# Retention and mixture of experts on one core: ten chunks whole in place of nine, and a five-step lead for the first expert job

## Chip, cores and metric

The kernel runs on one core of a Trainium2 chip. The metric is the device time of one execution in microseconds (us), as the median of several runs; lower is better. A profile is one further execution, taken by the hardware profiler.

## What is computed

A retention layer (a decaying linear attention) over 4 sequences of 768 tokens with 8 heads of 64 features is followed by a mixture of experts: each of the 3072 tokens goes to the one of 8 experts that its logits choose, through two matrix products with a ReLU between them.

```python
for t in range(S):                       # retention, per batch b and head h
    state = gamma * state + outer(k[:, :, t], v[:, :, t])
    y[:, :, t] = scale * q[:, :, t] @ state
x = y as [3072, 512]                     # heads side by side
logits = x @ w_gate + modality_bias[modality_id]
e_idx = argmax(logits);  gate_w = softmax(logits)[e_idx]
for e in range(8):
    h = relu(x[mask_e] @ w1[e])          # 512 -> 1024
    out[mask_e] = gate_w * (h @ w2[e])   # 1024 -> 512
```

## The kernel before

**Retention in chunks.** The 3072 tokens are 24 chunks of 128 tokens, six to a sequence (`NN` = 24, `NCH` = 6). A chunk needs the masked scores of its keys and queries, the state that earlier chunks left, the outputs from both, and the state for the next chunk. There are two forms:

- *Whole* (chunks 0 to 8, `n < WHOLE`, line 42): `whole_scores` (lines 281 to 290) makes 128x128 scores into two banks of PSUM, `whole_masked` masks them with two VectorE operations, `whole_state` (300) adds all 128 tokens to the state and copies it out with ScalarE (`keep_state`, 267), and `whole_out` (316) makes the output, again in two banks, and copies it as `yT` with two ScalarE operations. In matmul instructions of the trace that is 16 for scores, 16 for state, 16 for the state's part of the output (line 322) and 16 for the values' part (328): 64 a chunk.
- *In halves* (chunks 9 to 23): `scores`, `masked`, `grown` and `quarters` (211 to 378) treat two halves of 64 tokens, with matmuls of 64x64 on the four quarters of the array through `run` (line 276): 128 matmul instructions a chunk. One VectorE operation masks the scores, the state is copied out twice, and the output once.

The two forms lay the state out differently. `hand_over` (338) moves it with 16 matmul instructions on an identity (line 344) at the border, and copies the result out with ScalarE. The inputs are laid out on the host to the form of each chunk, and `decay_v` (1054) picks the factors for it. After either form `tokens_out` (381) transposes the output back to tokens (PE, line 388), and scales it: three VectorE operations (`lh`, `xs`, `lh`, line 396), one for the logits (`lg`, 417), and four on ScalarE (410).

**Routing.** After every third chunk `route` (1070) puts small steps on a list `todo`; `tick` (1066) runs one of them. For the second group of chunks (3 to 5) the steps are `a`, `a1`, `wait`, `first_b`, `wait`, `c`, `d`. Step `c` ends in the VectorE operation `ohs` (711); step `d` multiplies `ohs` on TensorE (`pt`, 721), and VectorE writes the list of jobs (`lst`, 725). From that list SyncE reads which rows and which expert the first job has.

**Jobs.** A job takes 256 tokens of one expert. Each weight tile is cut into a high part (ScalarE, `hi`, line 813) and a low part (VectorE, `lo`, 815). The rows are transposed on TensorE (`flip_x`; `xp`, 857) and split into `xTh` (ScalarE, 827) and `xTl` (VectorE, 828). Then come 96 matmuls of the first layer (872) and 48 of the second (887). Between them a job advances retention by five steps.

**Order of work.** PE, ScalarE, VectorE and SyncE run what the program issues in the order of the Python code. The generator `retention` (1140) yields three times in a whole chunk (after the next chunk's scores; after the tokens of the chunk before; at the end), twice in chunk 6, and twice in a chunk in halves. The main loop `everything` (1202) calls `tick` after each yield. At the first yield of chunk 8 the first list is written, and the first job is started there: loads of its rows and weights are issued. From then on the loop counts down:

```python
            if ahead is None:
                if min(EVENTS) in lists:
                    job = state_of[0] = start_job(jobs[0])
                    raw(job, 1, guess)
                    raw(job, 2)
                    ahead = AHEAD
            else:
                ahead -= 1
                if ahead in (2, 3):
                    cut(job, 1, 3 - ahead)
                if ahead == 1:
                    flip_x(job)
                if ahead == 0:
                    break
```

After the break the jobs run. The first layer's weights of a guessed expert are loaded earlier (from 29.8 us); `raw(job, 1, guess)` loads them again only if the guess was wrong.

Of the kernel before, what the change touches and what calls it, by code (L numbers as in the profile page):

```python
# [36 lines left out]

RUN = 8

AHEAD = 4  # L40

WHOLE = 9
EMPTY = 2 * NCAND
ZROW = NE * NT

# [10 lines left out]
def kernel(  # L56
# [194 lines left out]
    def grown(n, u):  # L251

        c = n % NCH
        if c == 0 and u == 0:
            pst[n // NCH] = bank(f"st_{n}")[:, : NG * D].rearrange("p (g e) -> p g e", g=NG)
        p = pst[n // NCH]
        kk = kvs[n][:, 0].rearrange("p (u g d) -> p u g d", u=2, g=NG)
        vd = values(n)
        return [
            (  # L260
                p[rows(j), g], kk[rows(j), u, g], vd[rows(j), u, g],
                c == 0 and u == 0 and g == 0,
            )
            for g in range(NG) for j in range(2)
        ]

    def keep_state(n, u):

        s = sts[n, u] = wk.tile([P, NG, D], F32, tag="s", name=f"s{u}_{n}", bufs=3)
        b = (n - 1 + u) // NCH  # L270
        nc.scalar.copy(s, pst.pop(b) if u and n % NCH == NCH - 1 else pst[b])

    def run(*lists):
        for i in range(0, max([0] + [len(l) for l in lists]), 2):
            for out_, l, r, start in sum((l[i : i + 2] for l in lists), []):
                nc.tensor.matmul(out_, l, r, start=start, stop=True, skip_group_check=True)  # L276
# [4 lines left out]
    def whole_scores(n):  # L281
        kt, qt = feat(n, 0), feat(n, 1)
        p = [bank(f"sc{j}_{n}").rearrange("p (g t) -> p g t", g=NG) for j in range(2)]
        for g in range(NG):
            for j in range(2):
                nc.tensor.matmul(  # L286
                    p[j][:, g], kt[rows(j), g], qt[rows(j), g], start=True, stop=True,
                    skip_group_check=True,
                )
        psc[n] = p  # L290

    def whole_masked(n):
        p = psc.pop(n)
        att[n] = me.tile([P, 2, NG, P], F32, tag=f"hi1{2 + n % 2}", name=f"a_{n}")
        for j in range(2):
            nc.vector.tensor_tensor(  # L296
                att[n][:, j], p[j], mask.unsqueeze(1).to_broadcast([P, NG, P]), op=ALU.mult
            )

    def whole_state(n):  # L300
# [11 lines left out]
        keep_state(n + 1, 0)  # L312
        if c == NCH - 2 and n + 1 < WHOLE:
            pst.pop(n // NCH)
# [690 lines left out]
    def raw(s, m, old=None):  # L1005
        load_weights(m, s["e"], None if old is None else old["e"])
# [47 lines left out]
    def decay_v(n):  # L1054
        vv = kvs[n][:, 1].rearrange("p (h e) -> p h e", h=H)
        by = decw if n < WHOLE else dec
        vds[n] = wk.tile([P, H, D], F32, tag="vd", name=f"vd_{n}", bufs=3)
# [82 lines left out]
    def retention(modi):  # L1140
# [5 lines left out]
        for n in range(NN):  # L1146
            if n < WHOLE:
                if (n + 1) % NCH:
# [4 lines left out]
                if listed:  # L1153

                    tokens_out(*prev)
                    route(min(EVENTS))
                if n + 1 < WHOLE:
                    whole_scores(n + 1)
# [5 lines left out]
                yield n  # L1164
                if n + 1 < WHOLE:
                    whole_masked(n + 1)
                else:
                    masked(n + 1)
                if prev is not None and not listed:
                    tokens_out(*prev)  # L1170
                    if n % GRP == 0:
                        route(n // GRP - 1)
                if n + 1 == WHOLE:
                    run(grown(n + 1, 0))
# [27 lines left out]
    def everything():  # L1202
# [17 lines left out]
        for n in ret:  # L1220
# [4 lines left out]
# [7 lines that stand above are left out]
# [141 lines left out]
```

## Time and profile before

| | us |
|---|---|
| median of 3 runs | 419.12 (417.92 to 419.55) |
| the profiled execution | 420.01 |
| its span in the trace | 418.2 |
| PE busy | 400.0 |
| VectorE (DVE) busy | 251.7 |
| ScalarE (ACT) busy | 207.3 |
| GpSimd (POOL) busy | 91.6 |

Times in the rows are us from the start of the span, unless marked ns. PE is TensorE, DVE VectorE, ACT ScalarE, POOL GpSimd, SP SyncE. The chain of waits follows the work that ended last back through what released it. "issue" is time in which the engine waited for nothing that the profile shows. PEclk is the TensorE clock that was granted: 1.00 is 2.4 GHz, 0.50 is 1.2 GHz.

### The profile page before, as it was taken

Reading aid. Unit: us, or ns where it says so; the run is one execution under the profiler, and the core shown is the slowest. Engines: PE = TensorE matmul, PEld = TensorE weight load, DVE = VectorE, ACT = ScalarE, POOL = GpSimd, SP = SyncE. Lnnn points to the kernel's source line nnn. Section 1 sums busy time; section 2 is a strip of 40 time slices with the busy share of each in tenths; the row PEclk is TensorE's granted clock in tenths of the full one; section 3 lists DMA queues with packets and bytes.
Section 4 is the critical chain, followed back from the end, with each engine's and each line's share of the span. In section 5 each row is a group of like instructions: output and inputs, shape, how many; then the busy total and the mean of one; then the engine's idle time right before and its main releaser. Section 6 shows DMA issues by size and latency. Waiting matters only on the chain.

```text
span 418.2 us, 12000 instructions
## 1 busy us (share of the span) xinstructions
PE 400.0 (96%) x4598; PEld 349.8 (84%) x4598; DVE 251.7 (60%) x605; ACT 207.3 (50%) x420; POOL 91.6 (22%) x118
## 2 busy tenths in 40 slices
PE   4998899999999999999999999999999999999994
PEld 3886799789879988988888988989898898968863
DVE  1876868746735767647745865967665573725600
ACT  1344276466545553655446537546454654626411
POOL 2425301412041115012501231210130101002001
PEclk9999899999999999999999999999999999999998
DMA  8999569986977664436920414842287589999001
GB/s 282 390 410 360 165 214 385 394 293 225 340 232 266 246 229 154 150 113 203 348 75 28 153 38 148 256 165 78 76 276 265 194 274 309 333 409 351 4 0 46
DMA packets 29978, 92.78 MB, mean 222 GB/s; under 512 B 4827, under 2 KB 4955, under 8 KB 29857
## 3 DMA queue, kind: packets, MB, share of 16 engines
q1 hardware_dynamic: 25360, 77.83, 53.7%
q0 software_dynamic: 4272, 13.67, 8.4%
q8 instruction: 37, 0.61, 0.6%
q10 hardware_dynamic: 288, 0.50, 0.3%
q14 instruction: 21, 0.17, 0.1%
HBM read 92.74 MB, written 17.48 MB: 264 GB/s over the span
## 4 chain that ended last, share of the span: by engine, by line
PE 82%; issue 8%; DMA 4%; DVE 3%; POOL 1%; POOLq 0%; ACT 0%; SPq 0%; ACTq 0%
PE h_e L872 28%; PE o_e L887 27%; PE x L388 6%; PE sc L276 3%; PE st L276 3%; PE h_s L872 3%; PE y L276 2%; PE xp_e L857 2%; DMA four<-in_w_dram 2%; PE sc L286 2%; PE y L328 2%; DMA cst<-in_consts_dram 1%; DVE a L296 1%; PE st L308 1%; PE y L322 1%
## 5 line engine op out<-in xcount | busy, mean ns | idle before, releaser
L815 DVE TENSOR_TENSOR lo_e<-raw,hi_e 128x1024 fp32r<-128x1024 f32 x80 | 100.7, 1260 | 72.9 <-ACT hi_e L813 65.3
L872 PE MATMUL h_e<-xTh,hi_e 128*128 128x256 f32 x320 | 91.9, 287 | 0.0
L872 PE MATMUL h_e<-xTh,lo_e 128*128 128x256 f32 x320 | 90.3, 282 | 0.0
L872 PE MATMUL h_e<-xTl,hi_e 128*128 128x256 f32 x320 | 90.3, 282 | 0.0
L813 ACT CAST hi_e<-raw 128x1024 fp32r<-128x1024 f32 x80 | 83.6, 1047 | 0.0
L887 PE MATMUL o_e<-hi_e,hTh 128*128 128x512 f32 x160 | 66.1, 413 | 0.0
L887 PE MATMUL o_e<-lo_e,hTh 128*128 128x512 f32 x160 | 63.2, 395 | 0.0
L887 PE MATMUL o_e<-hi_e,hTl 128*128 128x512 f32 x160 | 63.1, 394 | 0.0
L872 PEld LDWEIGHTS h_e<-xTh,hi_e 128*128 128x128 f32 x320 | 60.7, 190 | 0.7
L872 PEld LDWEIGHTS h_e<-xTh,lo_e 128*128 128x128 f32 x320 | 60.6, 189 | 0.3
L872 PEld LDWEIGHTS h_e<-xTl,hi_e 128*128 128x128 f32 x320 | 60.7, 190 | 0.0
L1058 POOL TENSOR_TENSOR vd<-kv,cst 128x512 f32<-128x512 f32 x24 | 28.2, 1174 | 99.6 <-DMA kv<-in_qkv_dram 40.4
L822 ACT ACTIVATE hTh<-h_e 128x256 fp32r<-128x256 f32 x80 | 30.8, 387 | 29.9 <-PE h_e L872 25.6
L410 ACT ACTIVATE xs<-x,cst 128x64 f32<-128x64 f32 x96 | 22.3, 315 | 45.2 <-DVE lh L396 26.0
L900 POOL DMA_INDIRECT out_dram<-o_e,xg_e x20 | 19.9, 994 | 112.2 <-ACT o_e L899 95.8
L823 DVE SCALAR_TENSOR_TENSOR hTl<-h_e,hTh 128x256 fp32r<-128x256 f32 x80 | 33.0, 419 | 14.3 <-ACT hTh L822 14.2
L887 PEld LDWEIGHTS o_e<-lo_e,hTh 128*128 128x128 f32 x160 | 30.1, 188 | 7.1
L899 ACT ACTIVATE o_e<-o_e,xg_e 128x512 f32<-128x512 f32 x20 | 13.8, 690 | 43.9 <-issue 27.3
L887 PEld LDWEIGHTS o_e<-hi_e,hTh 128*128 128x128 f32 x160 | 30.1, 188 | 6.1
L887 PEld LDWEIGHTS o_e<-hi_e,hTl 128*128 128x128 f32 x160 | 30.2, 189 | 5.5
L494 POOL DMA_INDIRECT x_dram<-xs,pos x24 | 26.9, 1119 | 33.9 <-DVE xs L460 12.8
L388 PE MATMUL x<-wgt,yT 128*128 128x144 f32 x192 | 31.2, 306 | 2.4 <-issue 1.8
(214 smaller groups left out, 659.5 us busy)
## 6 DMA issues: line engine op xcount, KB each, us to landing
raw<-in_w_dram SPq DMA_DIRECT2D x100, 512.0 KB
kv<-in_qkv_dram SPq DMA_DIRECT2D x24, 512.0 KB
four<-in_qkv_dram SPq DMA_DIRECT2D x19, 512.0 KB
xg_e<-x_dram SPq DMA_DIRECT2D x20, 257.0 KB
four<-in_w_dram SPq DMA_DIRECT2D x8, 512.0 KB
wb_u<-in_w_dram SPq DMA_DIRECT2D x16, 256.0 KB
kq<-in_qkv_dram SPq DMA_DIRECT2D x4, 512.0 KB
xg_s<-x_dram SPq DMA_DIRECT2D x4, 257.0 KB
```

The costliest lines, as they stand in the source:

```text
L276: nc.tensor.matmul(out_, l, r, start=start, stop=True, skip_group_check=True)
L388: nc.tensor.matmul(px[:, g], yT[:, 2 * u + g], wgt[:, 2 * u + g], start=(g == 0), stop=(g == 1), skip_group_check=True,)
L410: nc.scalar.activation(x[:, i], px[:, i // 2, rows(i % 2)], AF.Copy, scale=gain[:, c, 4 * u + i : 4 * u + i + 1],)
L494: ins = nc.gpsimd.indirect_dma_start(out=x_dram[:, :], out_offset=bass.IndirectOffsetOnAxis(ap=pos[:, i : i + 1], axis=0), in_=xs, in_offs ...
L813: nc.scalar.copy(hi, raws[m][i])
L815: nc.vector.tensor_tensor(lo, raws[m][i], hi.bitcast(F32), op=ALU.subtract)
L822: nc.scalar.activation(hi, src, AF.Relu)
L823: nc.vector.scalar_tensor_tensor(lo, src, 0.0, hi.bitcast(F32), op0=ALU.max, op1=ALU.subtract)
L872: nc.tensor.matmul(ph, s["w1"][f // 2][wi][:, o : o + P], s["xT"][kc // 2][a][:, kc % 2, :], start=(n == 0), stop=(n == 3 * KC - 1),)
L887: nc.tensor.matmul(po, hT[f][a][:, hh * P : (hh + 1) * P], s["w2"][f // 2][wi][:, (f % 2) * DM : (f % 2 + 1) * DM], start=(n == 0), stop=( ...
L900: ins = nc.gpsimd.indirect_dma_start(out=out[:, :], out_offset=bass.IndirectOffsetOnAxis(ap=xg.bitcast(I32)[:, DM : DM + 1], axis=0), in_= ...
L1058: ins = nc.gpsimd.tensor_tensor(vds[n], vv, by[:, n % NCH].unsqueeze(2).to_broadcast([P, H, D]), op=ALU.mult)
```

## The change

Two constants change. Chunk 9 is computed whole, so that `hand_over` and the first scores in halves come at the end of chunk 9 and concern chunk 10; the inputs' layout and the decay factors follow. The count from the first list to the first job is five steps in place of four. Since a whole chunk has three yields and one in halves two, the first job still begins after the last yield of chunk 9.

```diff
-AHEAD = 4
-
-WHOLE = 9
+AHEAD = 5
+
+WHOLE = 10
```

In the order of the code the stretch from the scores of chunk 9 to the first job changes as follows (what VectorE and ScalarE do is in brackets):

```
before: scores(9) in halves, hand_over(9) [ACT s, s], d, [DVE lst, masked(9)], tokens 7, grown(9,0) [ACT s],
        [cut 0], whole_out(8) [ACT yT], [cut 1], quarters(9) first part [ACT s], flip_x [xTh, xTl],
        quarters(9) second part [ACT s, yT], [masked(10)], tokens 8, [a], job 0
after:  whole_scores(9), d, [DVE lst, masked(9) twice], tokens 7, whole_out(8) [ACT yT], [cut 0],
        whole_state(9) [ACT s], scores(10) in halves, hand_over(10) [ACT s], [cut 1], [masked(10)], tokens 8,
        grown(10,0) [ACT s], [a], flip_x [xTh, xTl], whole_out(9) [ACT yT], [a1], job 0
```

## Rows read from the trace of the kernel before

**Rows 1.** The page: span, and the TensorE clock in 40 slices.
```profile
span 418.2 us, 12000 instructions
PEclk9999899999999999999999999999999999999998
```

**Rows 2.** Waits of PE from 60 to 366 us: what waited, for what, total, times, longest.
```profile
PE y L276 <- issue: 1.2, 3, 0.4
```

**Rows 3.** Chain of waits, 40 to 60 us: start, duration, engine and line.
```profile
46.52 0.78 PE sc L276 x21
...
49.64 1.12 PE st L344 x16
50.76 0.14 PE pt L721 x3
50.91 2.18 PE x L388 x8
...
56.25 1.02 PE xp_e L857 x8
...
58.37 1.18 PE x L388 x8
59.55 0.47 PE h_e L872 x4
```

**Rows 4.** The same chain, 16 to 22 us: whole chunks alone.
```profile
17.09 0.46 PE st L308 x16
17.55 1.09 PE sc L286 x16
...
19.82 0.60 PE y L322 x16
20.42 1.02 PE y L328 x16
```

**Rows 5.** Busy time in stretches of 1 us, then PEclk, DMA share, GB/s.
```profile
48.00:49.00 1.00, 0.28 (x2) 0.19 (x2) 1.00 (x1) 0.36 (x2) 0.98 (x2) 1.00 0.41 152
49.00:50.00 1.00, 0.82 (x13) 0.67 (x14) 0.52 (x1) 0.37 (x1) 0.48 (x1) 0.75 0.68 239
...
52.00:53.00 1.00, 1.00 (x5) 0.78 (x4) 0.52 (x2) 0.00 (x0) 0.00 (x0) 0.54 0.55 205
```

**Rows 6.** Timeline of DVE: start, duration, line, operation; in brackets idle before.
```profile
47.72 1.80 DVE L711 TENSOR_SCALAR ohs<-ord_r,rank,full 96x2 bf16<-96x2 f32 x1
...
58.49 1.27 DVE L828 TENSOR_TENSOR xTl<-xp_e,xTh 128x512 fp32r<-128x512 f32 x2
59.69 0.67 DVE L221 TENSOR_TENSOR a<-sc,cst 128x512 f32<-128x512 f32 x1
...
60.72 0.17 DVE L396 TENSOR_TENSOR lh<-x,cst 128x32 f32<-128x32 f32 x1
...
64.82 1.22 DVE L815 TENSOR_TENSOR lo_e<-raw,hi_e 128x1024 fp32r<-128x1024 f32 x1
```

**Rows 7.** Timeline of ACT, the same columns.
```profile
50.87 0.37 ACT L271 COPY s<-st 128x256 f32<-128x256 f32 x1 [1.28 <-PE st L344]
53.40 0.93 ACT L410 ACTIVATE xs<-x,cst 128x64 f32<-128x64 f32 x4 [2.16 <-DVE lh L396]
...
54.59 1.05 ACT L813 CAST hi_e<-raw 128x1024 fp32r<-128x1024 f32 x1
55.55 0.64 ACT L334 COPY yT<-y 128x256 f32<-128x256 f32 x2
...
57.29 1.10 ACT L827 CAST xTh<-xp_e 128x512 fp32r<-128x512 f32 x2
```

**Rows 8.** Timeline of POOL.
```profile
48.42 1.06 POOL L1058 TENSOR_TENSOR vd<-kv,cst 128x512 f32<-128x512 f32 x1
```

**Rows 9.** Timeline of SP: DMA issues.
```profile
54.50 1.82 SPq L809 DMA_DIRECT2D raw<-in_w_dram x4
```

**Rows 10.** All instructions of line 711: duration in ns as min/median/max, first and last start.
```profile
L711 DVE TENSOR_SCALAR ohs<-ord_r,rank,full x5: 286/289/1800, 47.7 to 241.6; 96x2 bf16<-96x2 f32 x5
```

## The prediction

> **What bounds the kernel now.** I read the page first, then the waits of PE, then the chain of waits around the code that changes, and last the timelines of the other engines there. The span is 418.2 us, and the granted clock is at its full 2.4 GHz in all slices but the fifth, which holds the stretch of this change, and the last [rows 1]. From 60 to 366 us PE waits for no other engine: the largest entry is pauses marked "issue", 0.4 us each [rows 2]. So the time is PE's stream, and whatever moves the start of the first job moves the end by as much. That start is the first h_e matmul at 59.55 us [rows 3]; up to the scores of chunk 9 at 46.52 nothing changes. Thus the question is how long the new order takes from 46.52 to job 0, where the old one takes 13.03 us.
>
> In those 13 us the reader is to see two losses of the kernel before. The scores of chunk 9 in halves begin at 46.52, but hand_over only at 49.64 [rows 3]; 21 of the 32 matmul instructions took 0.78 us, so all would take 1.19, and the rest is pauses. And after PE had little to do (0.28 of 48 to 49 us) its clock is 0.75 in the mean of 49 to 50 and 0.54 in that of 52 to 53, which is half clock from 49.5 to about 52.9 [rows 5]: the eight matmul instructions of tokens 7 took 2.18 us, where those of tokens 8 took 1.18 [rows 3].
>
> **The matmuls of the change.** Chunk 9 whole costs 1.09 for scores, 0.46 for state, and 0.60 and 1.02 for the output: 3.17 us [rows 4]. In halves it has 128 instructions, and the 64 of the second part of quarters(9) run from 57.27 (56.25 + 1.02) to 58.37 [rows 3], 1.10 us, so 2.2 us in all. On PE the change therefore adds about 1.0 us. hand_over (1.12) is moved, not added.
>
> The Trainium skill (TensorEngine Tiling (Array Packing), Theoretical Speedup) speaks against the change too: with both dimensions at most 64 the array works as four tiles at once. By that, as an estimate from its counts, 128 instructions of 64 columns on four tiles are 2048 column steps, and the whole form has 3584 on two, a ratio of 1.75 where the rows give 3.17/2.2 = 1.44. The sum would then be 0.6 us later on PE; the measured ratio decides, and PE is not what comes last below.
>
> **Step d is reached too early.** Its pt matmuls need ohs, which DVE ends at 47.72 + 1.80 = 49.52 [rows 6]. Before, pt came at 50.76, behind hand_over, and did not wait. Now only the whole scores stand ahead of it, and they end at 46.52 + 1.09 = 47.61. PE stands 1.9 us, and behind pt in its queue are tokens 7, whole_out(8) and all the rest. Only the order after ohs changes on DVE, and the POOL copy that overlaps it (48.42 to 49.48 [rows 8]) stays too; so I keep 49.52. The other bound is the median of ohs, 0.29 [rows 10], an end at 48.01.
>
> The Trainium skill (SBUF — State Buffer, Who interferes with whom) says that DVE and GpSimd lock a pair of ports for a whole instruction, and the loser blocks. By that rule ohs stood until the POOL copy ended; the rows agree (49.52 against 49.48). By it the wait remains in the changed kernel, and without it the sum would be that of rival 4.
>
> Does the clock fall again? PE idles from 47.61 to 49.6, about as little work as before in that stretch, and before it fell to half right after. No row shows which of the two it will be here; the nearest, [rows 5], says it falls. I take that, and keep the other end.
>
> Then pt 49.6 to 49.75; tokens 7, 2.18, to 51.9; whole_out(8), 1.62 at full clock, has its first 1.0 us at half clock and ends at 54.1; the yT copies (0.64 [rows 7]) end at 54.85. Without the fall they end later than PE alone would give, behind tokens 7 on DVE and ACT: three small operations with lst (0.17 each, as lh) and two maskings (2 x 0.67) from 49.8, then three small operations (0.5), 0.93 and 0.64 on ACT [rows 6, 7]: 53.7.
>
> **From the first cut to the first job.** Cut 0 now stands behind yT(8), so it begins at 54.85 (or 53.7). Its weights' flag is no obstacle: it came 3.6 us after pt (50.9 to 54.50 [rows 3, 9]), so now at 53.35. The price of the change lies behind it, since whatever is issued between cut 0 and flip_x stands ahead of the split of x. Before, only yT(8), cut 1 and one state copy stood there. Now, one after the other, each waiting for the one ahead of it: hi of cut 0 (1.05) and the copy of s (0.37) on ACT; hand_over(10) on PE (1.12), which reads that copy; the copy of its result (0.37); hi of cut 1 (1.05); on DVE lo of cut 1 (1.22), masked(10) (0.67) and three operations of tokens 8 (0.5, from the end of masking to the second lh); on ACT the four of tokens 8 (0.93) and the state copy behind grown(10,0) (0.37); then the first xTh (0.55, half of 1.10) [rows 3, 6, 7]. These are 8.2 us; 54.85 + 8.2 = 63.05. xTl adds 0.63 for each half and is read by the third and the ninth matmul of the job, which holds the first twelve another 0.3 us: the job begins, in effect, at 63.4 in place of 59.55. **That is 3.85 us later.** If the clock doesn't fall, cut 0 is at 53.7 and the delay 2.7.
>
> PE is earlier than that: after 54.1 come state 0.46, scores(10) 1.19 (to 55.75), a wait for the copy of s (to 56.2), hand_over 1.12, tokens 8 1.18, grown 0.6, flip_x 1.02 and whole_out(9) 1.62, to 61.75 [rows 3, 4]. So PE waits there 1.3 us, and the extra microsecond of matmuls is hidden beneath the chain; if that cover goes, PE alone costs 61.75 - 59.55 = 2.2 (with no fall of the clock 1.1).
>
> **At no cost.** The second masking operation ends long before DVE's next late work: after tokens 7 DVE waits for the first hi until 55.9. If that cover went, it would cost 0.67. The decay copies on POOL are the same. The loads on SP stand in the same order; load_kv(12) is issued behind the same weight loads. Group 2's routing starts one tick earlier (a1 before job 0 rather than in it): about 1.3 us of DVE that PE doesn't read at once. Weight loads of job 0 are issued 1.1 us earlier, but PE waited for none of them. In job 0 and after, the order is as before, so nothing there gives time back. The few pauses marked issue fall in code in halves [rows 2], and one group of them, over 1 us, may come or go anywhere: plus or minus 1.3 us.
>
> **Rivals.**
> 1. *The clock falls a second time*, since PE stands 1.3 us just before job 0. For it: [rows 5], half clock after little work. Against: the stretch there is shorter than the 1.9 us ahead of pt. Half clock for the same 3.4 us costs 1.7 more: 5.55 later, 424.7.
> 2. *PE's stream comes last*, because ACT and DVE overlap more than my chain lets them. 1.1 to 2.2 later: 420.2 to 421.3.
> 3. *Nothing waits and the time does not rise*: ohs is there in time, the clock holds, and the chain hides. The place is the gap from 47.6 to 49.6. Then PE has 1.09 + 0.14 + 1.18 + 1.62 + 0.46 + 1.19 + 1.12 + 1.18 + 0.6 + 1.02 + 1.62 = 11.2 us from 46.52, to 57.75: 1.8 earlier, 417.3. It decides if ohs ends by 47.6 and xTh by 57.7. Against it: ohs has even its short duration only at 48.0, and the chain is 8.2 us long from cut 0.
> 4. *ohs takes 0.29*: all is 1.5 us earlier and the clock holds. Cut 0 then follows its flag, 48.15 + 3.6 = 51.75, and the job begins at 60.3: 0.75 later, 419.9.
> 5. *The change does not do what it says*: the job begins at another step. The yields speak against that: three in each of chunks 8 and 9, counted from the first of chunk 8, leave five; one step more or less would move half a chunk (1.1 us) to the other side of the job's start without adding to PE's work. I give it no chance of its own.
>
> **How the numbers follow.** The profiled execution has 420.01; plus 3.85 that is 423.86. It stood 0.89 above the median, so the forecast is 419.12 + 3.85 = 423.0. Chances: this forecast 0.40; the same without the fall of the clock (421.8) 0.15; rival 1 0.14; rival 2 0.12; rival 3 0.12; rival 4 0.07. About 0.5%, or 2.1 us, is what a measurement of this kernel tells from no change: slower is above 421.2, faster below 417.0. Forecast, its milder form and rival 1 give slower, less 0.04 for pauses that vanish: 0.65. Faster needs rival 3 and a pause less, half of its chance: 0.06. The rest, 0.29, is no change. The range reaches from rival 4 less 0.3 to rival 1 plus a pause's half: 419.6 to 425.4; outside lie rival 3 and the tails.
>
> **What would show it.** In the profile after: PE idle from 47.6 to about 49.6 ahead of pt, for ohs; a clock of 0.50 after it; the first hi of job 0 near 54.9, and hand_over just behind the copy of s; the first h_e near 63 with PE waiting for xTh; and from there the same PE stream with no wait on another engine, shifted by about 4 us. The prediction is wrong if pt does not wait, if h_e begins before 61.2, or if later jobs give time back.

## The result and the profile after

The changed kernel takes 420.29 us in the median (419.76 to 421.33) against 419.12 (417.20 to 419.73) for the kernel before, measured beside it: a ratio of 1.0036 [1.0023, 1.0049]. It is slower, by 1.2 us where 3.85 was forecast; by the limit of 2.1 us that the prediction set itself, this counts as no change. A later comparison gave 420.04 against 418.34, 1.0044 [1.0027, 1.0061], so 1.7 us.

The profiled execution of the changed kernel has 421.33 and a span of 419.5. The page's two lines that answer to [rows 1]:

```profile
span 419.5 us, 11869 instructions
PEclk9999969999999999999999999999999999999998
```

The waits of PE from 10 to 366 us (waited for, total, times, longest):

```profile
PE st L344 <- ACT s L271: 3.3, 1, 3.3
PE pt L721 <- DVE ohs L711: 2.0, 1, 2.0
PE x L388 <- ACT yT L334: 0.6, 1, 0.6
```

All three stand ahead of job 0. pt waits for ohs and hand_over (344) for a copy on ScalarE, as the prediction has it. But the pauses marked "issue" of [rows 2] are gone: from 66 us on PE has no entry at all.

The chain of waits, 55 to 68 us (start, duration), answers to [rows 3]:

```profile
55.58 0.07 DMA raw<-in_w_dram
...
55.67 1.04 ACT hi_e L813
56.72 0.28 ACT s L271
...
57.04 1.12 PE st L344 x16
58.16 2.22 PE x L388 x8
60.38 1.05 PE st L276 x16
61.43 1.51 PE xp_e L857 x8
62.94 0.60 PE y L322 x16
63.54 1.02 PE y L328 x16
64.56 3.06 PE h_e L872 x24
```

Cut 0 waits for its weights, the copy of s and hand_over follow it, and job 0 begins at 64.56. Tokens 8 took 2.22 us here and 1.18 in [rows 3], so half clock lies there.

**Where the time went.** I divide each execution at one mark in job 0, the first matmul of its second layer (o_e, line 887). Ahead of it lies all that the change touches; what precedes `ohs` isn't touched either, so the stretch is counted from the start of `ohs`. The timeline of PE gives the mark, first for the kernel before and then for the changed one:

```profile
75.94 0.50 PE L887 MATMUL o_e<-hi_e,hTh 128*128 128x512 f32 x1
```
```profile
81.38 0.50 PE L887 MATMUL o_e<-hi_e,hTh 128*128 128x512 f32 x1
```

Between these two executions the stretch grew from 28.2 (75.94 - 47.72 [rows 6]) to 34.0 us (81.38 - 47.36), and the rest of the span shrank from 342.3 to 338.1. A loss larger than forecast, and a gain of 4.2 that no step of the prediction has, net 1.3. The experiments ask what each of the two is.

### The profile page after: what moved, and what is told of

It reads as the page before. It is cut to its first block, busy times and chain, and to the rows that moved or that the text cites. A ratio compares the mean times of both kernels' runs of the same rounds, so it can differ in the third digit from the quotient of the medians.

```text
span 419.5 us, 11869 instructions
## 1 busy us (share of the span) xinstructions
PE 401.3 (96%) x4534; PEld 351.5 (84%) x4534; DVE 251.7 (60%) x606; ACT 206.9 (49%) x420; POOL 91.8 (22%) x118
## 4 chain that ended last, share of the span: by engine, by line
PE 75%; issue 7%; DMA 2%; POOL 1%; POOLq 0%; ACT 0%
PE h_e L872 28%; PE o_e L887 27%; PE x L388 5%; PE st L276 3%; PE h_s L872 3%; PE sc L276 3%; PE xp_e L857 2%; PE y L276 2%; DMA four<-in_w_dram 2%; POOL out_dram L900 1%; PE uh_u L945 0%; POOL out_dram L974 0%; PE o_s L887 0%; POOLq L914 0%; PE st L344 0%
## 5 line engine op out<-in xcount | busy, mean ns | idle before, releaser
L815 DVE TENSOR_TENSOR lo_e<-raw,hi_e 128x1024 fp32r<-128x1024 f32 x80 | 99.1, 1239 | 76.0 <-ACT hi_e L813 75.8
L822 ACT ACTIVATE hTh<-h_e 128x256 fp32r<-128x256 f32 x80 | 30.8, 388 | 31.4 <-PE h_e L872 26.7
L823 DVE SCALAR_TENSOR_TENSOR hTl<-h_e,hTh 128x256 fp32r<-128x256 f32 x80 | 33.0, 418 | 14.6 <-ACT hTh L822 14.4
L899 ACT ACTIVATE o_e<-o_e,xg_e 128x512 f32<-128x512 f32 x20 | 13.8, 690 | 42.6 <-issue 23.6
L494 POOL DMA_INDIRECT x_dram<-xs,pos x24 | 26.9, 1120 | 34.0 <-DVE xs L460 12.8
L815 DVE TENSOR_TENSOR lo_s<-raw,hi_s 128x1024 fp32r<-128x1024 f32 x16 | 19.5, 1222 | 21.0 <-ACT hi_s L813 20.5
```

Source lines behind the costliest of these rows:

```text
L494: ins = nc.gpsimd.indirect_dma_start(out=x_dram[:, :], out_offset=bass.IndirectOffsetOnAxis(ap=pos[:, i : i + 1], axis=0), in_=xs, in_offs ...
L815: nc.vector.tensor_tensor(lo, raws[m][i], hi.bitcast(F32), op=ALU.subtract)
L822: nc.scalar.activation(hi, src, AF.Relu)
L823: nc.vector.scalar_tensor_tensor(lo, src, 0.0, hi.bitcast(F32), op0=ALU.max, op1=ALU.subtract)
```

## Experiments

The executions that follow, divided at the same mark (us, each from its own trace; "pauses" are the issue pauses of PE behind the mark; a group, below, is a set of kernels that ran together):

| execution | ohs begins | first o_e | ohs to o_e | o_e to end | pauses |
|---|---|---|---|---|---|
| before | 47.72 | 75.94 | 28.2 | 342.3 | yes |
| before_2 | 46.10 | 77.47 | 31.4 | 338.1 | no |
| before_3 | 46.85 | 77.91 | 31.1 | 338.2 | no |
| before_4 | 46.03 | 77.38 | 31.4 | 338.3 | no |
| after | 47.36 | 81.38 | 34.0 | 338.1 | no |
| after_2 | 46.01 | 80.65 | 34.6 | 338.2 | no |
| after_3 | 46.42 | 79.73 | 33.3 | 338.1 | no |
| after_4 | 47.57 | 81.30 | 33.7 | 338.1 | no |
| b_shift64 | 46.91 | 75.95 | 29.0 | 337.9 | no |
| a_shift64 | 46.39 | 80.60 | 34.2 | 338.0 | no |
| a_kv_late | 47.52 | 78.45 | 30.9 | 338.2 | no |
| a_cuts_late | 46.85 | 80.32 | 33.5 | 338.1 | no |
| a_kv_flip | 46.52 | 75.98 | 29.5 | 338.1 | no |
| b_kv_late_2 | 47.00 | 73.90 | 26.9 | 338.2 | no |
| b_kv_late | 49.04 | 77.36 | 28.3 | 341.1 | yes |
| b_lead5 | 48.54 | 82.55 | 34.0 | 337.0 | yes |
| a_flip_early | 47.54 | 76.78 | 29.2 | 341.0 | yes |
| a_kv_cuts_late | 48.98 | 84.76 | 35.8 | 341.0 | yes |
| a_kv_flip_vd | 48.66 | 80.06 | 31.4 | 340.5 | yes |

Names with b_ are variants of the kernel before, with a_ of the changed one.

**Is the gain of 4.2 us the change's?** One theory: the pauses hang on places in PE's instruction stream, and the change, with 128 fewer instructions on PE, moved them away. Then 64 tiny matmuls at the start of either kernel should move them too, and bring them to the changed one or take them from the one before.

```diff
+    def dummies(count):
...
+        for _ in range(count):
+            nc.tensor.matmul(spare[:1, :1], nul, nul, start=True, stop=True, skip_group_check=True)
...
     def retention(modi):
+        dummies(64)
         whole_scores(0)
```

> The kernel before with 64 tiny matmuls of one column (128 instructions on PE with their weight loads) ahead of the first scores, where PE waits for the first load until about 5.3 us; nothing else changes. In the trace of before, PE has four groups of pauses marked issue (47, 81, 116 and 204 us), all in code in halves; in the trace after, which has 128 PE instructions fewer from chunk 9 on, there is none. Theory A (place in the instruction stream: the pauses hang on where code in halves stands in PE's stream of instructions, and 128 instructions more or less move them away): the groups at 81, 116 and 204 us are gone or stand in other places, and if they are gone the time is 3 to 4 us below before, about 415.5. Theory B (the pauses hang on what else moves at that time, and it was the later start of job 0 that moved them): they stay where they are, and the time is that of before, 419.1 +- 0.7.

> The changed kernel with the same 64 tiny matmuls at the start, so that from chunk 10 on every PE instruction has the number in the stream that it had in the kernel before. Theory A: the groups of pauses come back near the same instructions as in before (in the jobs at about 85, 118 and 206 us here), and the time is 3 to 4 us above the changed kernel, about 424. Theory B: no pauses, 420.3 +- 0.7.

b_shift64 took 417.02, 0.9962 [0.9947, 0.9978], and a_shift64 420.42, 1.0046 [1.0024, 1.0069]. Neither has a pause behind the mark. The first alone would have fitted the theory, the second not. (b_shift64 is all the same faster than the kernel before, and that comes from ahead of the mark, which is 29.0 us behind `ohs`: PE waits 2.5 us for the first job's rows where the kernel before, below, waits 3.2 to 3.5, and its clock stays full from 44 to 83 us. Why is not shown.) So both kernels were run again without an edit.

> The kernel before, unchanged, one more profiled execution. In the first one PE had four groups of pauses marked issue (47, 81, 116, 204 us), and TensorE's clock was at 1.2 GHz from 49.5 to 52.9. Theory C (pauses and falls of the clock belong to the single execution): other places or none, a span of 414 to 418 us, and without pauses the first h_e near 57.5 to 59. Theory D (they belong to this kernel): the same groups within 1 us, 418.2 +- 0.5.

> The kernel before once more. Theory C: again another set of pauses and falls than in the other two. Theory D: the same as in both.

> The changed kernel, unchanged, one more profiled execution. The first had no pauses, one fall of the clock from 55.6 to 62.4 and its first h_e at 64.56. Theory C: another fall of the clock or none; with none the first h_e is near 62 and the span near 417, and pauses may show in the jobs. Theory D: 419.5 +- 0.5 with the same fall.

> The changed kernel once more. Theory C: the wait of PE for ohs (2.0 us) and the wait of hand_over are there in every execution, since they come from the order of the code; the clock and the pauses differ. Theory D: all the same.

They took 417.42, 417.92, 420.62 and 419.63. The kernel before has no pauses either, and its rest is 338.1 and 338.2 us, to 0.1 that of the changed kernel. The theory falls: the 4.2 us are no effect of the change. Set beside before_2, o_e matmul by o_e matmul, before falls back 1.0, 1.8 and 1.3 us at its three groups of pauses behind the mark, and nowhere else. All six executions with pauses, of kernels with and without the 128 instructions, also have a longer one of 1.3 to 1.4 us ahead of `ohs`, in before this one:

```profile
36.44 0.76 PE L388 MATMUL x<-wgt,yT 128*128 128x144 f32 x4 [1.38 <-issue]
```

The short ones come in the scores of chunk 9 where that chunk is in halves, and behind it mostly near 81, 116 to 126 and 204 to 213 us. Of the kernels of one group all profiled executions have pauses or none has, and the kernel before took 420.44 and 420.31 in the two comparisons with pauses, 418.06 to 418.46 in the three without. What brings them stays open.

The waits of PE in before_2, 10 to 366 us:

```profile
PE xp_e L857 <- DMA xg_e<-x_dram: 3.5, 2, 2.8
PE st L344 <- ACT s L271: 1.1, 1, 1.1
PE x L388 <- ACT yT L334: 0.6, 1, 0.6
PE pt L721 <- DVE ohs L711: 0.2, 1, 0.2
...
```

This is not the kernel of [rows 2] and [rows 3]: flip_x waits 3.5 us for the rows of job 0, a wait that the profiled execution of the kernel before does not have. Without pauses, then, the change moves the mark from 31.3 (mean of three) to 33.9 us (mean of four) behind ohs: 2.6 us, and nothing after it. The changed kernel was not run in a group with pauses, so what the change costs there is not known.

**What makes the rows late?** SyncE's DMA queue in before, before_2 and after (issue, duration, what):

```profile
41.29 8.30 SPq L120 DMA_DIRECT2D kv<-in_qkv_dram  x2
52.59 0.90 SPq L838 DMA_DIRECT2D xg_e<-x_dram  x2
```
```profile
39.47 5.85 SPq L120 DMA_DIRECT2D kv<-in_qkv_dram  x2
52.19 1.83 SPq L838 DMA_DIRECT2D xg_e<-x_dram  x2
```
```profile
40.73 5.85 SPq L120 DMA_DIRECT2D kv<-in_qkv_dram  x2
53.67 0.90 SPq L838 DMA_DIRECT2D xg_e<-x_dram  x2
55.58 1.82 SPq L809 DMA_DIRECT2D raw<-in_w_dram  x4
```

The second of the two kv loads (chunk 11) ends its issue at 49.6 in the first (41.29 + 8.30), and at 45.3 and 46.6 in the others. It waits for the state of chunk 8, and goes out right behind it in the others but some 2.7 us behind it in the first, as in a_flip_early and b_lead5 below, which have pauses too. In a_flip_early it can't be pauses of PE that hold it: PE has none there between 37 and 115 us. In before_2 the row load then waits for rows on their way to `x_dram`; SyncE's waits, 42 to 62 us, have this line, and the chain of waits of before_2 these:

```profile
SPq L838 <- DMA x_dram<-xs,pos: 2.4, 1, 2.4
```
```profile
45.81 6.36 DMA x_dram<-xs,pos
...
52.75 3.48 DMA xg_e<-x_dram
...
56.27 1.73 PE xp_e L857 x7
```

In after the same wait is 2.6 us, and in the ten executions without pauses and with this load in its place it is 1.9 to 2.9. So the theory is that the kv load, issued just before the last scatter, holds the scatters up and with them the row load and all that SyncE issues behind it. The test puts that load behind the row load.

```diff
-                load_kv(n + 7 if n < 3 else n + 3)
+                if n != 8:
+                    load_kv(n + 7 if n < 3 else n + 3)
...
                 yield n
+                if n == 8:
+                    load_kv(11)
```

> The changed kernel with the load of kv for chunk 11 issued behind the first job's rows and weights in place of ahead of them. In the trace after, the load of the job's rows waited until 53.67 us for the scatters of rows, where in the trace before it went out 1.6 us after the list; the kv load went out at 46.2 in the one and at 49.3 in the other. If the kv transfer holds up the scatters, the rows are loaded near 51.3, the flag of the weights comes near 53.3 and the first hi at 53.3 in place of 55.67, and job 0 begins about 2 us earlier: 418.3. If the scatters land late for another reason, the row load stays at 53.5 and the time at 420.3.

> The kernel before (nine chunks whole) with the load of kv for chunk 11 issued behind the first job's rows and weights. In two further executions of the kernel before, without pauses, PE waits 3.2 to 3.5 us at the transposition for the job's rows, whose load waits 2.4 to 2.8 us for the scatters of rows; in the changed kernel the same delay of the kv load brought the rows 2 us nearer to the list. Theory (this wait, not PE's stream, sets the start of job 0 in most executions of the kernel before): it goes, job 0 begins 2 to 3 us earlier, ratio about 0.994, some 416 us. Rival (the first profile was typical, and rows are in time): no difference, 1.000 +- 0.002.

> The kernel before with the load of kv for chunk 11 behind the job's rows and weights, again. If the call has no pauses: the wait for rows at the transposition (3.2 to 3.5 us) goes, ratio 0.993 to 0.996 if it set the start of job 0, 1.000 if something else is as late. With pauses: 1.000, as before.

a_kv_late: 418.19 where a_shift64 beside it had 420.42, and 1.0005 [0.9986, 1.0025] to the kernel before. b_kv_late: 420.34, 0.9999 [0.9985, 1.0014], which tells nothing, since its group had the pauses and with them a late kv load anyway (28.3 from ohs to o_e, and 28.2 in the profiled execution of the kernel before). Repeated in a group without them, b_kv_late_2: 413.90 (413.31 to 414.54), 0.9900 [0.9874, 0.9925]. It is the shortest of all, faster than both kernels. Its DMA queue and its waits of PE, 10 to 366 us:

```profile
50.69 0.88 SPq L838 DMA_DIRECT2D xg_e<-x_dram  x2
```
```profile
PE st L344 <- ACT s L271: 1.1, 1, 1.1
...
PE xp_e L857 <- DMA xg_e<-x_dram: 0.2, 1, 0.2
...
```

The wait for rows fell from 3.5 to 0.2, and the scatters themselves land sooner. The DMA issues of 42 to 60 us, in before_2 and then in b_kv_late_2, end in the median us from issue to landing:

```profile
x_dram<-xs,pos POOLq DMA_INDIRECT x3, 6.4
```
```profile
x_dram<-xs,pos POOLq DMA_INDIRECT x3, 3.7
```

It is 5.9 to 6.9 in the ten executions named above and 3.7 to 3.9 in the three without pauses that have the load moved. So that the load holds up the scatters, and these the rows, is shown in both kernels; how it holds them up is not. Moving one load takes the mark from 31.3 to 26.9 us in the kernel before and from 33.9 to 30.9 in the changed one. With rows in time the change costs 30.9 - 26.9 = 4.0 us, by a single trace of each. Part of the gain is the clock: before_2 has half clock behind its wait for rows (0.56 in the mean of 56 to 59 us), while b_kv_late_2 and a_kv_late have full clock from 44 to 83 us.

**What comes last in the changed kernel?** The prediction says the cuts and what stands between them and the split of x. Cutting behind the handed-over state, directly ahead of flip_x, takes them out of hand_over's way:

```diff
-                if ahead in (2, 3):
-                    cut(job, 1, 3 - ahead)
                 if ahead == 1:
+                    cut(job, 1, 0)
+                    cut(job, 1, 1)
                     flip_x(job)
```

> The changed kernel with both cuts of job 0 issued together, just ahead of its transposition, behind hand_over, the masking of chunk 10 and the tokens of chunk 8. My theory (the delay of job 0 to 64.6 us is the chain first cut, copy of s, hand_over, second cut, masking, tokens, split of x on ScalarE and VectorE): hand_over no longer waits for the flag of the weights, so it runs near 53.7 in place of 57.0, PE does not stand 3.3 us and its clock need not fall; the first h_e is near 61 and the time 3 us below the changed kernel, about 417.3. Rival (PE's own stream, with a fall of the clock, is the limit): the first h_e stays above 63.5 and the time within 1 us of 420.3.

418.68, 1.0008 [0.9991, 1.0024]; a_shift64 beside it has 1.0046. hand_over no longer waits (3.3 us in after), and the first h_e stands 13.8 us behind ohs where the four executions of the changed kernel have 15.8 to 17.1. But PE now waits 0.8 for xTh and 1.1 for xTl, the clock falls again there (0.66 in the mean of 62 to 65 us), and the mark shows only 0.4 us (33.9 to 33.5) of the 1.7. The gain goes with the clock: the profiled run, 420.24, and four others with a mean clock of 0.987 to 0.991 took 419.08 to 420.37, the five with 0.994 to 0.997 took 417.33 to 418.27. The reverse is to bring the split of x forward by one step:

```diff
-                if ahead == 1:
+                if ahead == 2:
                     flip_x(job)
```

> The changed kernel with the transposition and split of the job's rows right behind the second cut, ahead of the masking of chunk 10 and the tokens of chunk 8. If masking and tokens stand in the chain to job 0 (by the durations 0.67 + 0.5 on VectorE and 0.93 + 0.37 on ScalarE), the split is ready 2 to 2.5 us earlier, PE no longer waits for xTh, and the time falls by 1.5 to 2: about 418.5. If PE's own stream is last, 420.3 +- 0.7.

> The changed kernel with kv of chunk 11 behind the job's rows, and the transposition and split of the rows ahead of masking and tokens. Both parts of the chain to job 0 are shorter (2 us by the rows, 2 to 2.5 by masking and tokens), and PE's own stream comes last: job 0 about 12 to 13 us after the state matmuls of chunk 8, ratio to the kernel before 0.993 to 0.997 without pauses, 0.998 to 1.000 with them. Rival: the clock falls in the wait for ohs and eats it, ratio above 1.001.

a_flip_early, in a group with pauses: 421.31, 1.0029 [1.0014, 1.0043]; the mark is 29.2 behind ohs, and PE does not wait for xTh. (The profiled run, 419.62, is the shortest of its eleven, and the changed kernel was not in that group, so what this edit gains alone can't be told.) a_kv_flip has the kv load moved as well, without pauses: 415.54, 0.9936 [0.9913, 0.9959]. PE has two waits left in 10 to 366 us:

```profile
PE pt L721 <- DVE ohs L711: 2.0, 1, 2.0
PE x L388 <- ACT yT L334: 0.6, 1, 0.6
```

The mark is at 29.5, where a_kv_late has 30.9: 1.4 us is what the split of x lost behind masking and tokens 8, at the least, since a_kv_flip has half clock on the way (0.50 at 50 to 53 us) and a_kv_late has not; by the medians of two groups it is 2.65 (418.19 - 415.54). Two more mix the edits:

> The changed kernel with both edits that gained alone: kv of chunk 11 behind the job's rows, and both cuts of job 0 behind hand_over, masking and tokens. If the two losses (the late rows, and hand_over behind the first cut) are separate parts of the chain, the gains add in part: about 417, some 3 us below the changed kernel and 1.5 below the kernel before. If cuts late on ScalarE have become the chain themselves, the earlier rows bring nothing more: 418.5, as with the late cuts alone.

> The second half of the change alone: nine chunks whole, but the first job five steps behind its list. The job begins behind the first half of chunk 10, and PE has that work, tokens 8 and masking while the rows are on their way. If the kernel before waits for rows in most executions, the wait of 3.2 to 3.5 us at the transposition shrinks to below 1 and the ratio is about 0.995. If the chain of cuts, masking and tokens takes its place, as in the changed kernel, PE waits for the split of x instead and the ratio is 1.000 to 1.004.

a_kv_cuts_late: 427.6, 1.0174 [1.0150, 1.0197]. One group of pauses fell ahead of its mark (2.3 us more there than a_cuts_late) and the others behind it (2.9 more), so the time can't tell whether the two gains add. Up to the first h_e they don't: it stands 13.8 us behind ohs, as in a_cuts_late, though the rows are loaded 1.6 us earlier (4.1 behind ohs, and 5.7). b_lead5 is the kernel before with `AHEAD = 5` alone, in the same group: 420.57, 0.9991 [0.9973, 1.0009]. PE waits 1.1 us for xTh there as well:

```profile
62.84 0.39 PE L872 MATMUL h_e<-xTh,hi_e 128*128 128x256 f32 x1 [1.13 <-ACT xTh L827]
```

A fifth step by itself changes nothing there that can be measured: the mark is later (34.0) and the rest the shortest of all (337.0, with pauses), as half a chunk more is done ahead of the job. And the split of x comes last there without a tenth chunk made whole. Ten whole chunks with a lead of four were not run.

**Does ohs wait for GpSimd?** The decay copy of chunk 10 was queued behind a small GpSimd operation that needs what is computed from ohs, in a_kv_flip:

```diff
+        if g == 1:
+            junk = small("junk", [NCAND, 1])
+            ins = nc.gpsimd.tensor_tensor(junk, keep, keep, op=ALU.mult)
+            held.append(getattr(ins, "ins", ins))
...
+        with tc.issue_after(held[0]) if n == 10 else nullcontext():
```

> The kernel a_kv_flip with GpSimd's decay copy for chunk 10 held until the list is written (a tiny operation on GpSimd that reads what VectorE writes just behind the list, and the copy queued behind it). If the copy holds ohs: ohs ends at 48.1 in place of 49.2 (at the end of the last scatter's issue) or at 47.7 (its 0.29 us of other places), PE's wait for ohs falls from 2.0 to 0.5 to 0.9 us, list and rows come 1.1 us earlier if the scatters have landed, and the time falls by 0.5 to 1 us. If ohs takes 1.8 us for another reason, it ends where it did, and time and wait stay.

The timelines of DVE and GpSimd in a_kv_flip_vd:

```profile
48.66 0.29 DVE L711 TENSOR_SCALAR ohs<-ord_r,rank,full 96x2 bf16<-96x2 f32 x1
```
```profile
48.38 0.97 POOL L494 DMA_INDIRECT x_dram<-xs,pos  x1 [0.30 <-issue]
...
50.89 1.04 POOL L1065 TENSOR_TENSOR vd<-kv,cst 128x512 f32<-128x512 f32 x1
```

and in after:

```profile
47.36 1.81 DVE L711 TENSOR_SCALAR ohs<-ord_r,rank,full 96x2 bf16<-96x2 f32 x1
```
```profile
48.06 1.07 POOL L1058 TENSOR_TENSOR vd<-kv,cst 128x512 f32<-128x512 f32 x1
```

With the copy gone from beside it ohs takes 0.29 us in place of 1.81, though a scatter is still under way on GpSimd, and PE's wait for it falls from 2.0 to 0.4. Whether it bought time can't be told: 421.81, 1.0046 [1.0024, 1.0068], comes from a group with pauses in which a_kv_flip was not run. The rows still came late (SyncE waits 1.7 us for the scatters, and 0.6 in a_kv_flip), and hand_over waits for s behind cut 0:

```profile
PE st L344 <- ACT s L271: 3.4, 1, 3.4
```

Last, both kernels unedited once more, beside b_kv_late_2 and a_kv_flip:

> The kernel before, one more profiled execution, to see whether the executions of this call have PE's pauses (job 0 near 13 us after the state matmuls of chunk 8, rows in time) or not (job 0 near 16 us after them, PE waiting over 3 us for rows).

> The changed kernel beside the kernel before in this call. If the call has no pauses: job 0's first matmul about 17 us after the state matmuls of chunk 8, 1 us or so behind the kernel before, and further waits in its first products, ratio 1.004 to 1.006. With pauses in both: the kernel before starts job 0 3 us earlier relative to that point, but loses more in its first pause, ratio 1.002 to 1.004. If the forecast's 59.55 was the usual start, the ratio is 1.009.

417.52 in its one execution, and 420.04, 1.0044 [1.0027, 1.0061]; the table has their places, like those of before_2, before_3, after_2 and after_3.

## Why the prediction was right or wrong, point by point

**The sign is right, and the forecast size is that of another case than the one measured.** The 3.85 us are the loss of a kernel whose rows come in time. With them in time in both kernels (b_kv_late_2 and a_kv_late) the loss is 4.0 us by the mark, and 1.0005 - 0.9900 of 418.5, 4.4 us, by the medians of two groups. That the forecast meets this is in part luck: it counts on a fall of the clock that neither of these traces has (without it the prediction says 2.7), and it has the first h_e 11.8 and 15.3 us behind the start of ohs, where they have 10.3 and 13.5; the rest of their 4.0 is lost between the first h_e and the mark. In the kernels as they stand the rows are late: that costs the kernel before 4.4 us (26.9 to 31.3) and the changed one, which waits for other things at that time, only 3.0 (30.9 to 33.9). Hence 2.6: the first h_e moves from 14.6 to 16.4 us behind ohs in the mean, 1.8, and 0.9 more is lost between it and the mark.

**The step that failed is the first: the old start at 59.55 [rows 3].** It comes from an execution with pauses, in which the kv load went out late and so let the rows land early. (What delayed it stays open. The delay of 2.7 us comes with pauses in three traces, in one of them with no pause of PE near it, and the profile calls the load's last releaser "remote".) The same pauses cost 4.2 us in the jobs, so that its time, 420.01, looked ordinary. The sign was on the page: it stood above all three timed runs, and pauses stood in the very stretch that I costed [rows 3]. I priced the pauses at plus or minus 1.3 as a nuisance of code in halves, though the longest, 1.38 us, stands in the tokens of a whole chunk, and did not ask what else is different where they are. By the trace of before_2 the old start is at 61.08, 14.98 behind ohs, where the prediction has 11.83. None of the three signs of being wrong that the prediction names came (pt waited, h_e began behind 61.2, no job gave time back): none of them tests the old start.

**pt waits for ohs: right.** 2.0 us, forecast 1.9. Also that the POOL copy does it: 0.29 us without it. Rivals 3 and 4 are out: the copy stayed, and PE has this wait of 2.0 us in all four executions of the changed kernel.

**The flag at 53.35, "3.6 us after pt": wrong, for the same cause.** The weights' loads stand behind the row load on SyncE, which waits for the scatters. The first hi begins at 55.67, 8.3 us behind the start of ohs (8.0 to 8.6 in the four executions), where the forecast has 7.1. In a_kv_late it begins at 53.25 (5.7 behind ohs): there the flag is no obstacle.

**The chain of 8.2 us: right.** The timeline of ACT in after, which answers to [rows 7]:

```profile
55.67 1.04 ACT L813 CAST hi_e<-raw 128x1024 fp32r<-128x1024 f32 x1 [2.52 <-DMA raw<-in_w_dram]
56.62 0.37 ACT L271 COPY s<-st 128x256 f32<-128x256 f32 x1
58.27 0.37 ACT L271 COPY s<-st 128x256 f32<-128x256 f32 x1 [1.28 <-PE st L344]
58.53 1.05 ACT L813 CAST hi_e<-raw 128x1024 fp32r<-128x1024 f32 x1
62.05 0.93 ACT L410 ACTIVATE xs<-x,cst 128x64 f32<-128x64 f32 x4 [2.47 <-issue]
62.85 0.39 ACT L271 COPY s<-st 128x256 f32<-128x256 f32 x1
63.11 0.26 ACT L433 ACTIVATE ex<-lg 128x24 f32<-128x24 f32 x1
63.23 1.10 ACT L827 CAST xTh<-xp_e 128x512 fp32r<-128x512 f32 x2
```

Cut 0 at 55.67, first xTh done near 63.8: 8.1 us, in the order that was forecast. Only `ex`, a step of the next group's routing, was not on the list; it begins before the first xTh and adds about 0.1. In after_2, after_3 and after_4 the same chain takes 7.7 us, since hand_over takes 0.69 there: the 1.12 of [rows 3], which the prediction takes as its price, is its time at half clock, and so it is in after.

**PE is not last: half right.** In after PE's own stream came last: h_e follows whole_out(9) with no wait. Half clock lay on tokens 8 and flip_x there. In after_3 that stretch ran at full clock, and PE waits 1.3 us for xTh, as forecast. a_shift64 and a_kv_late show the same 1.3. The two limits lie close: in after the first xTh is done 0.7 us before h_e begins, in after_3 PE is done 1.3 us before it. So which of the two comes last differs between executions of one program, and where PE does (after, after_4) half clock lies on its stream, which is not the overlap that rival 2 names. (The 0.6 us that the prediction gives by the count of columns comes out at 0.7, 2.2 x (1.75 - 1.44); nothing hangs on it.)

**The clock: right that it falls, wrong that the place can be told.** The busy time in stretches of after, then of after_3 (length; PE, PEld, DVE, ACT and POOL busy; PEclk; DMA share; GB/s):

```profile
50.00:53.00 3.00, 3.00 (x66) 2.62 (x66) 1.87 (x6) 1.31 (x6) 0.62 (x1) 1.00 0.40 154
...
56.00:59.00 3.00, 1.96 (x20) 1.84 (x21) 1.23 (x1) 1.72 (x4) 0.00 (x0) 0.50 0.32 88
59.00:62.00 3.00, 3.00 (x25) 2.61 (x25) 2.35 (x5) 0.58 (x1) 0.00 (x0) 0.50 1.04 355
```
```profile
50.00:53.00 3.00, 3.00 (x44) 2.67 (x36) 0.93 (x5) 1.57 (x6) 0.52 (x1) 0.50 0.08 26
...
59.00:62.00 3.00, 2.07 (x37) 1.49 (x34) 2.25 (x9) 1.48 (x7) 0.00 (x0) 1.00 0.93 324
```

The same program has half clock behind the wait for ohs in one execution (0.50 at 50 to 53 in after_3), and in the other full clock there and half from the wait of hand_over on (0.50 at 56 to 62 in after). after_2 has it twice (0.57 at 50 to 53 and 0.64 at 62 to 65), as rival 1 has it, and its stretch is the longest (34.6). Behind the wait for ohs, 1.9 to 2.0 us in ten executions with ten whole chunks, the clock fell in six, where ohs starts at 46.0 to 46.9 or at 49.0 us, and held in the four where it starts at 47.4 to 47.6: the wait alone does not decide it.

**No later job gives time back: right.** The rest is 338.1 to 338.3 in all seven executions of the two kernels without pauses. The shorter rest that the first pair of traces shows was the pauses.

**What stays open.** What brings the pauses. And why the profiles differ by 2.6 us where the timed medians differ by 1.2 to 1.7: the three later profiles of the kernel before lie at 417.42 to 417.92 with medians of 418.06 to 419.12, and two of the four of the changed kernel are the longest of their series (421.33 and 421.19), so part of it may be which executions were profiled; no run shows it. Some timed runs of the first comparison may have had pauses; they left no trace, so that stays open too.

## What to carry to other kernels

Before a start is read from a trace, set the profiled execution's time against the timed runs, and where it lies outside them or shows pauses that nothing explains, ask what else is different in that execution: here a wait of 3.5 us was missing from the trace. A bulk load issued just ahead of scatters on which a later load waits is worth moving behind that load; here it made the kernel before 1.0% faster in a group without pauses, 0.9900 [0.9874, 0.9925], and changed nothing in one with them (0.9999). And when a border is moved past a job's preparation, list what then stands on each queue between the first cut and the last split: that list (8.2 us forecast, 7.7 to 8.1 measured) held within 0.5 us in all four executions of the changed kernel.

## What the runs showed of the hardware

- A 96x2 operation on DVE took 1.81 us beside a GpSimd copy of 1.07 us and 0.29 with the copy moved away. The Trainium skill (SBUF — State Buffer, Who interferes with whom) says that, where operations of both use the shared pair of ports, one holds it for a whole instruction and the other blocks; the runs agree in the effect. The recorded start of ohs (47.36) is earlier than that of the copy (48.06), so which of them took the ports first the rows don't tell.
- One kv load of 512 KB issued ahead of the last of three scatters goes with a landing time of 5.9 to 6.9 us (median) for the scatters and a wait of 1.9 to 2.9 us for the load that depends on them, in ten executions. With it moved behind that load, the landing took 3.7 to 3.9 and the wait was at most 0.6 in three executions without pauses (1.7 in a_kv_flip_vd, which has pauses).
- The granted clock fell to half at different places in executions of one program, 50 to 53 us in one and 56 to 62 in another, at either of two waits of PE; the same wait of 2.0 us brought a fall in some executions and none in others.
- Pauses of PE of about 0.4 us each, with one of 1.3 to 1.4 us ahead of them, came in all profiled kernels of one group of runs or in none, and cost 2.4 to 4.2 us behind the mark (340.5 to 342.3 against 338.1).
